# A scheduler for two attentions on one core: opening the next accumulator early, issuing VectorE's score banks on their own, and measured times for VectorE and its shared port

## The chip, the cores and the metric

The kernel runs on one core of one Trainium2 chip. The time is the device time of that core in microseconds (us). The core's engines run side by side: PE (TensorE) multiplies matrices, ACT (ScalarE) takes exponentials, DVE (VectorE) and POOL (GpSimd) do elementwise work, and SP issues DMAs. A program on a single core can be sorted into fast and slow runs only by the spread of its own times.

## The reference, cut to what matters

Two attentions of 32 heads of width 16 over 2048 positions, from separate inputs, joined along the last axis. A is causal within four segments of 512 and adds a memory of earlier segments; B attends to everything.

```python
# A, per segment s
p = softmax(einsum('bhqd,bhkd->bhqk', qs, ks) * scale + mask)
o = g * (phi(qs) @ M) / (phi(qs) @ z + 1e-6) + (1 - g) * (p @ vs)
M, z = M + phi(ks).T @ vs, z + phi(ks).sum()
# B
p = softmax(einsum('bhqd,bhkd->bhqk', q, k) * Dh ** -0.5)     # 2048 x 2048 for each of 32 heads
out = concat([o_A @ wo_A, (p @ v) @ wo_B], axis=-1)
```

B alone has 32 x 2048 x 2048 exponentials, so the work that counts is: scores on PE, their exponentials, and the product with V (P.V) on PE.

## The kernel before: the parts that matter

A score bank is 128 keys x 512 queries of one head in one PSUM bank; four heads (j = 0..3) make a block of keys. ACT takes the exponentials of tiles of 3 and 2 banks in turn. A unit is the work of one accumulator: four heads and 512 queries of one attention. Some blocks go to VectorE instead: one evacuation per bank (a linear map whose integer result is read as an fp16 bit pattern) and three more "rungs" of the same block with other offsets, all four of which are summed by P.V matmuls. A block that goes to VectorE costs it four evacuations and three rungs, costs PE three more quads of P.V, and takes four banks from ACT.

The program is laid out at build time by a scheduler that keeps an estimated clock for each engine (`T["pe"]`, `T["act"]`, `T["dve"]`, `T["pool"]`) and writes PE's and VectorE's instructions in the order that it thinks best. On the chip that order is fixed: an engine that meets an instruction whose input or buffer isn't ready waits, and what stands behind it waits too (in the profiles below, a 3.7 us wait of VectorE holds up the k bank behind it and with it PE). In the code, slack is the time that PE has until ACT needs its next scores, and backlog the work that VectorE still has before it, both as estimated.

```python
def v_scores(taken, lim=2):              # give score banks to VectorE
    n = 0
    while n < lim and backlog() < VBACK and free_slots(...) and v_pick():
        ...
        later(0.685, v_evac(u, kb, x, j, vt, not left), vt)

# main loop, in order of preference (cut)
if held_back(t) and now >= rel - 0.03:   # all pT buffers still wait for P.V
    forced[0] += 1
    if not pv(1): ...
if slack > 0.45 and backlog() < 0.35 and v_scores(set(), 1):   # VectorE's banks alone
    continue
...
def do_phik(wk, k, out, then=None):      # phi(k), transposed by DMA for the memory of A
    pk = wk.tile([P, W], BF16, name="phkT", tag="phkT")        # one buffer
    ...                                                        # VectorE writes it
    for kb in range(4):
        nc.sync.dma_start_transpose(ph[:, kb, :], pk[:, kb * P:(kb + 1) * P])
...
def half():                              # run inside a task that counts 0.72 us of VectorE
    fin_half(wk, st, e)
    if e == 0:
        sums_ok(wk, 0, 32, okm[:, 0:1], "a")      # three VectorE operations each, not counted
        sums_ok(wk, 32, 63, okm[:, 1:2], "b")
```

`sums_ok` checks that the softmax sums stayed in the range of the approximation; if not, an exact program runs instead.

## Time and profile before

| | before |
|---|---|
| time, median | 935.04 us, 3 runs (934.98 to 935.51) |
| span of the profiled run | 932.0 us |
| ACT busy | 891.3 us in 770 score tiles and 30 other instructions |
| VectorE busy | 759.4 us |
| blocks on VectorE | 111 (444 evacuations, 333 rungs) |

First the page of the kernel before: its busy times (with the share of the span and the number of instructions), and four of its groups of instructions. A group's line ends with its busy time, the mean of one instruction in ns, the idle time just before them, and what ended most of it.

```profile
PE 868.7 (93%) x7609; PEld 265.6 (28%) x7609; DVE 759.4 (81%) x1265; ACT 891.3 (96%) x800; POOL 170.1 (18%) x335
...
L774 ACT ACTIVATE pT<-s_ps 128x1536 bf16<-128x1536 f32 (+1 forms) x770 | 879.3, 1301 | 21.3 <-PE s_ps L104 10.8
L846 DVE TENSOR_SCALAR vx<-v_ps 128x512 uint16<-128x512 f32 x444 | 296.6, 686 | 90.5 <-PE v_ps L104 86.5
...
L858 DVE TENSOR_SCALAR vx<-vx 128x2048 uint16<-128x2048 uint16 x333 | 221.3, 708 | 1.9
...
L104 PE MATMUL acc<-zeros 128*128 128x512 bf16 x508 | 164.6, 386 | 0.0
```

PE looks as busy as ACT, but 508 of its matmuls are filler on zeros: the scheduler puts them where PE has nothing to do. ACT has 96% and nothing that could be left out. Where it idles is shown by the windows of the kernel before, for ACT (columns: stretch, its length, busy time and number of instructions, granted PE clock, DMA share, GB/s):

```profile
0.00:42.00 42.00, 21.48 (x21) 0.84 0.76 166
42.00:97.00 55.00, 54.71 (x51) 1.00 0.08 21
97.00:860.00 763.00, 759.02 (x680) 1.00 0.03 9
860.00:932.00 72.00, 56.09 (x51) 0.93 0.03 10
```

Length less busy time is idle time: 20.5 us while weights and first projections arrive, 0.3 us from 42 to 97 us, 4.0 us in the 763 us after that, and 15.9 us in the last stretch, most of it the tail after the last tile. ACT is the limit, so what the change is worth is the ACT time it removes, less the ACT idle time that it adds.

### The profile page before, as it was taken

What the parts mean: (1) busy time and instruction counts of PE and PEld (TensorE: products, weight loads), DVE (VectorE), ACT (ScalarE), POOL (GpSimd) and SP (SyncE); (2) the same over time, 40 slices, a digit from 0 to 9 for tenths busy, and PEclk for the clock granted to TensorE, in tenths of its full rate; (3) what the DMA queues carried; (4) which work ended last, traced back from release to release, by engine and by line L of the source; (5) the groups of instructions that cost most, each with busy time, mean ns of one, the idle gap of its engine ahead of it and who ended that gap; (6) DMA issues with size and microseconds to landing.
All of it is one profiled execution on the core that took longest, in us unless ns stands there. A gap on an engine that the chain in (4) does not pass through costs nothing.

```text
span 932.0 us, 18773 instructions
## 1 busy us (share of the span) xinstructions
PE 868.7 (93%) x7609; PEld 265.6 (28%) x7609; DVE 759.4 (81%) x1265; ACT 891.3 (96%) x800; POOL 170.1 (18%) x335
## 2 busy tenths in 40 slices
PE   7899999999999999999999999999999999999986
PEld 2222232233232222223322233222232222222221
DVE  2474798888888888898888988888898988887885
ACT  4799999999999999999999999999999999999985
POOL 3740141330303003030220303021030300000000
PEclk9799999999999999999999999999999999999998
DMA  8600000000000110000000000000000010000000
GB/s 182 135 13 18 13 4 10 18 13 1 3 5 13 41 24 7 2 1 7 2 6 2 26 27 2 1 2 1 1 1 2 13 34 2 1 1 1 1 1 27
DMA packets 35648, 15.46 MB, mean 17 GB/s; under 512 B 27360, under 2 KB 35552, under 8 KB 35552
## 3 DMA queue, kind: packets, MB, share of 16 engines
q1 hardware_dynamic: 33776, 13.78, 6.1%
q8 instruction: 61, 1.00, 0.4%
q10 hardware_dynamic: 1776, 0.40, 0.2%
q14 instruction: 35, 0.29, 0.1%
HBM read 4.20 MB, written 4.19 MB: 9 GB/s over the span
## 4 chain that ended last, share of the span: by engine, by line
ACT 53%; issue 24%; PE 14%; POOL 5%; DVE 3%; DMA 1%; SPq 1%; ACTq 0%; DVEq 0%; POOLq 0%
ACT pT L774 52%; PE acc L104 5%; PE s_ps L104 4%; POOL pT L784 4%; PE v_ps L104 2%; ACT ex L260 1%; PE k_ps L104 1%; POOL qB L240 1%; DMA w_a<-in_A_wv_dram 1%; PE q_ps L104 1%; DVE vx L846 1%; SPq L205 1%; DVE vx L858 0%; PE l_ps L104 0%; PE o_ps L104 0%
## 5 line engine op out<-in xcount | busy, mean ns | idle before, releaser
L774 ACT ACTIVATE pT<-s_ps 128x1536 bf16<-128x1536 f32 (+1 forms) x770 | 879.3, 1301 | 21.3 <-PE s_ps L104 10.8
L846 DVE TENSOR_SCALAR vx<-v_ps 128x512 uint16<-128x512 f32 x444 | 296.6, 686 | 90.5 <-PE v_ps L104 86.5
L104 PE MATMUL s_ps<-qB,KB 32*128 32x512 bf16 x1604 | 253.9, 383 | 28.3 <-ACT pT L774 22.1
L858 DVE TENSOR_SCALAR vx<-vx 128x2048 uint16<-128x2048 uint16 x333 | 221.3, 708 | 1.9
L784 POOL TENSOR_SCALAR_AFFINE_SELECT pT<-pT 128x256 bf16<-128x256 bf16 (+2 forms) x244 | 111.9, 490 | 345.4 <-ACT pT L774 344.5
L104 PE MATMUL acc<-vx,VB 128*32 128x512 f16 x1776 | 164.9, 385 | 5.0 <-DVE vx L858 4.7
L104 PE MATMUL acc<-zeros 128*128 128x512 bf16 x508 | 164.6, 386 | 0.0
L104 PE MATMUL acc<-pT,VB 128*32 128x512 bf16 x1604 | 159.0, 389 | 0.0
L104 PE MATMUL v_ps<-qB,KB 32*128 32x512 bf16 x444 | 157.0, 384 | 0.5 <-DVE vx L846 0.2
L104 PEld LDWEIGHTS <-KB 32*128 32x128 bf16 x2048 | 85.7, 91 | 243.5 <-issue 235.8
L104 PEld LDWEIGHTS <-VB 128*32 128x32 bf16 x3380 | 71.6, 94 | 150.3 <-issue 140.1
L104 PEld LDWEIGHTS <-zeros 128*128 128x128 bf16 x524 | 40.7, 98 | 96.0 <-issue 86.1
L240 POOL TENSOR_SCALAR qA<-qc,par 128x512 bf16<-128x512 bf16 x30 | 26.4, 894 | 214.6 <-DVE qc L238 214.6
L104 PE MATMUL s_ps<-qA,kA 32*128 32x512 bf16 (+3 forms) x512 | 53.5, 306 | 8.3 <-ACT pT L774 4.9
L333 DVE STREAM_TRANSPOSE tT<-acc 128x512 f32<-128x512 f32 x64 | 45.2, 707 | 8.4 <-PE acc L104 8.0
L104 PE MATMUL acc<-pT,vA 128*32 128x128 bf16 (+3 forms) x512 | 38.2, 315 | 6.0 <-DVE vA L280 2.7
L104 PEld LDWEIGHTS <-kA 32*128 32x128 bf16 x512 | 16.6, 92 | 52.2 <-issue 49.8
L238 DVE CAST qc<-q_ps 128x512 bf16<-128x512 f32 x31 | 21.3, 686 | 8.7 <-PE q_ps L104 8.1
L240 POOL TENSOR_SCALAR qB<-qc,par 128x512 bf16<-128x512 bf16 x32 | 24.9, 792 | 7.7 <-DVE qc L238 7.7
L408 DVE CAST osb<-o_ps 128x512 bf16<-128x512 f32 x28 | 19.2, 686 | 8.1 <-PE o_ps L104 7.1
L104 PE MATMUL v_ps<-w_a,xT_a 128*128 128x512 bf16 x64 | 20.0, 408 | 3.1 <-DMA w_a<-in_A_wv_dram 2.2
L280 DVE CAST VB<-v_ps 128x512 bf16<-128x512 f32 x16 | 11.0, 690 | 12.6 <-PE v_ps L104 12.6
(86 smaller groups left out, 421.7 us busy)
## 6 DMA issues: line engine op xcount, KB each, us to landing
out_dram<-osb SPq DMA_DIRECT2D x31, 128.0 KB, 1.7
w_b<-in_B_wqkv_dram SPq DMA_DIRECT2D x3, 512.0 KB, 5.1
phk<-phkT SPq DMA_TRANSPOSE x48, 2.4
w_a<-in_A_wv_dram SPq DMA_DIRECT2D x1, 512.0 KB, 7.2
wo_a<-in_A_wo_dram SPq DMA_DIRECT2D x1, 512.0 KB, 4.2
wo_b<-in_B_wo_dram SPq DMA_DIRECT2D x1, 512.0 KB, 5.1
w_a<-in_A_wk_dram SPq DMA_DIRECT2D x1, 384.0 KB, 8.6
w_a<-in_A_wq_dram SPq DMA_DIRECT2D x1, 384.0 KB, 9.2
```

Source lines behind the costliest of these rows:

```text
L104: return pin(nc.tensor.matmul(out, lhsT, rhs, **k))
L205: nc.sync.dma_start_transpose(t[:, cc, :], xs[name][ch * W:(ch + 1) * W, cc * P:(cc + 1) * P])
L238: pin(nc.vector.tensor_copy(qc[:], ps[:]))
L240: pin(nc.gpsimd.tensor_scalar(dst[:, e, :], qc[:], par[:, e:e + 1], 0.0, ALU.mult, ALU.add))
L260: pin(nc.scalar.activation(ex[:], src, ACT.Exp))
L280: pin(nc.vector.tensor_copy(dst, ps[:].rearrange("p (h d) -> p h d", d=DH)))
L333: pin(nc.vector.transpose(st["tT"][:, e].rearrange("p c d -> p (c d)"), acc[:]))
L408: pin(nc.vector.tensor_copy(osb[:], ps[:]))
L774: pin(nc.scalar.activation(pT[:, 0:n, :], pt[:, 0:n, :], ACT.Exp, scale=SCALE))
L784: pin(nc.gpsimd.affine_select(out=blk, in_=blk, compare_op=ALU.is_ge, fill=0.0, base=0, pattern=[[0, len(sls)], [1, P]], channel_multiplie ...
L846: pin(nc.vector.tensor_scalar(x[:, j, :], vt[:], XSCALE, float(LADDER[0]), ALU.mult, ALU.add))
L858: pin(nc.vector.tensor_scalar(p[:], x[:], float(off - LADDER[0]), 32767.0, ALU.add, ALU.min))
```

## The change

Its intent: find more room for blocks on VectorE. It has three parts. VectorE's banks may be issued in a PE group of their own as soon as there is 0.35 us of slack and up to 1.4 us of backlog (before: 0.45 and 0.35), with a deeper backlog (1.8 instead of 1.2) and three blocks ahead instead of two. A P.V of the next unit may open its accumulator before the present unit is done, when buffers are held up. The scheduler counts 0.055 us less of VectorE's occupancy than its latency, models the SBUF port that VectorE and GpSimd share, and no longer flushes the pending finishing steps when a unit ends. The diff, cut to its core:

```diff
-VBACK = 1.2
+VBACK = 1.8
+DVEEND = 0.055
-VAHEAD = 2
-VFROM = 9
+VAHEAD = 3
+VFROM = 8
+VALONE = 1.4
     def on_pool(us, ready):
-        T["pool"] = max(T["pool"], ready) + us
+        start = clear(max(T["pool"], ready), ports["dve"])
+        T["pool"] = start + us
+        ports["pool"].append((start, T["pool"]))
         def emit(t):
-            T["dve"] = max(T["dve"], t["ready"]) + t["us"]
+            start = begin(t)
+            T["dve"] = start + t["us"] - DVEEND
+            if t["port"]:
+                ports["dve"].append((start, T["dve"]))
         def unit_done(u):
-            if e == 0:
-                while nfin[0]:
-                    assert dve_force(1) or dve_force()
-        def pv(lim, force=False):
+        def pv(lim, force=False, over=False):
-                if not pv(1):
+                if not pv(1) and not pv(1, over=True):
-            if slack > 0.45 and backlog() < 0.35 and v_scores(set(), 1):
+            if slack > 0.35 and backlog() < VALONE and v_scores(set(), 1):
... (a second use of over; tT gated by a flag; the loop at the end; an unused way to GpSimd)
```

More of the change, by code (lines that the diff above doesn't have):

```diff
@@ L53 @@
 VNOM = 3.75
-VAHEAD = 2
-VFROM = 9
+VAHEAD = 3
+VFROM = 8
+VALONE = 1.4
+POOLMIN = 99
 LEAD = 2.5
@@ L90 @@
     slots, live = [0.0] * 3, [False]
-    held = dict(qc=0, ex=False, phi=deque())
+    ports = {k: deque(maxlen=8) for k in ("dve", "pool")}
+    held = {"tT": False, "ex": False, "qc": 0, "phi": deque()}
     def mm(out, lhsT, rhs, at=0.0, **k):
@@ L114, in on_act, with clear, later @@
         return T["act"] + ACTEND
+    def clear(at, spans):
+        for a, b in spans:
+            if a <= at < b:
+                at = b
+        return at
     def on_pool(us, ready):
-        T["pool"] = max(T["pool"], ready) + us
-    def later(us, f, src=None, prio=0, ready=None, ok=None):
+        start = clear(max(T["pool"], ready), ports["dve"])
+        T["pool"] = start + us
+        ports["pool"].append((start, T["pool"]))
+    def later(us, f, src=None, prio=0, ready=None, ok=None, port=False, rung=None):
         if not live[0]:
@@ L125, in later @@
         seq[0] += 1
-        tasks.append(dict(prio=prio, seq=seq[0], ready=ready, us=us, f=f, src=src, ok=ok))
+        tasks.append(dict(prio=prio, seq=seq[0], ready=ready, us=us, f=f, src=src, ok=ok, port=port, rung=rung))
     def palloc(pool, shape, name):
@@ L137, in mark @@
     def mark(key, at=None):
-        avail[key] = T["dve"] if at is None else at
+        avail[key] = T["dve"] + DVEEND if at is None else at
     const = ctx.enter_context(tc.tile_pool(name="const", bufs=1))
@@ L236, in evac @@
             qc = wk.tile([P, W], BF16, name="qc", tag="qc", bufs=2)
-            held["qc"] += phi is not None
             pin(nc.vector.tensor_copy(qc[:], ps[:]))
@@ L243, in evac @@
             if phi is not None:
+                held["qc"] += 1
                 def then():
@@ L269, in rest @@
             next_phi()
-        later(1.1, rest, ready=end)
+        later(1.0, rest, ready=end, port=True)
     def do_v(mp, w, xT, kb, dst, key=None):
@@ L331, in f @@
             if e == 0:
+                held["tT"] = live[0]
                 st["tT"] = wk.tile([P, 2, 16, 32], F32, name="tT", tag="tT")
@@ L335, in f @@
                 then()
-        later(0.72, f, acc)
+        later(0.72, f, acc, ok=lambda: "tT" in st if e else not held["tT"])
     def fin_mem(mp, wk, st, mbd, phi, e, then=None):
@@ L353, in fin_pair @@
         rr = rsum[:, ridx:ridx + 2, :].rearrange("p e (c o) -> p e c o", o=1)
-        yield 0.35 if name == "b" else 0.5
+        yield 0.35 if name == "b" else -0.5
         pin(nc.vector.reciprocal(rr, tT[:, :, :, DH:DH + 1]))
@@ L364, in fin_pair @@
         if aT is None:
-            yield 0.75
+            yield -0.75
             pin(nc.vector.tensor_tensor(o, tT[:, :, :, 0:DH], rr.to_broadcast(bc), op=ALU.mult))
         else:
-            yield 0.5
+            yield -0.5
             r2 = wk.tile([P, 2, 16, 1], F32, name="r2", tag="r2", bufs=2)
@@ L372, in fin_pair @@
             t1, t2 = tT[:, :, :, 0:DH], aT[:, :, :, 0:DH]
-            yield 0.7
+            yield -0.7
             pin(nc.vector.tensor_tensor(t1, t1, rr.to_broadcast(bc), op=ALU.mult))
-            yield 0.7
+            yield -0.7
             pin(nc.vector.tensor_tensor(t2, t2, r2[:].to_broadcast(bc), op=ALU.mult))
-            yield 0.7
+            yield -0.7
             pin(nc.vector.tensor_tensor(o, t1, t2, op=ALU.add))
@@ L605, with begin @@
         held.update(pk=0, ph=0)
-        vlive, nfin = [2], [0]
+        vlive, npool = [2], [0]
+        def begin(t):
+            at = max(T["dve"], t["ready"])
+            return clear(at, ports["pool"]) if t["port"] else at
         def emit(t):
             tasks.remove(t)
-            T["dve"] = max(T["dve"], t["ready"]) + t["us"]
+            start = begin(t)
+            T["dve"] = start + t["us"] - DVEEND
+            if t["port"]:
+                ports["dve"].append((start, T["dve"]))
             if t["src"] is not None:
                 i, _ = slot_of.pop(id(t["src"]))
-                slots[i] = T["dve"] + 0.05
+                slots[i] = T["dve"] + DVEEND + 0.05
             t["f"]()
@@ L624, in dve_run @@
                     return
-                at = min(max(T["dve"], t["ready"]) for t in el)
+                at = min(begin(t) for t in el)
                 if at > limit:
                     return
-                emit(min((t for t in el if t["ready"] <= at), key=lambda t: (t["prio"], t["seq"])))
+                emit(min((t for t in el if begin(t) <= at + 0.01), key=lambda t: (t["prio"], t["seq"])))
         def dve_force(cls=None):
@@ L633, in dve_force @@
                 return False
-            emit(min(el, key=lambda t: (max(T["dve"], t["ready"]), t["prio"], t["seq"])))
+            emit(min(el, key=lambda t: (begin(t), t["prio"], t["seq"])))
             return True
@@ L640, in fin_push @@
         def fin_push(g):
-            c = next(g)
-            nfin[0] += 1
             def step():
@@ L646, in step @@
                 if c is None:
-                    nfin[0] -= 1
+                    held["tT"] = False
                 else:
-                    later(c, step, prio=1, ready=T["dve"])
-            later(c, step, prio=1, ready=T["dve"])
+                    later(abs(c), step, prio=1, ready=T["dve"], port=c < 0)
+            step()
         def free_slots(at):
@@ L824, with v_scores @@
         vahead = [0]
-        def v_scores(taken, lim=2):
+        def v_scores(taken, lim=2, force=False):
             n = 0
-            while n < lim and backlog() < VBACK and free_slots(T["pe"] + (0.1 if taken else 0.0)) and v_pick():
+            while n < lim and (force or backlog() < VBACK) and free_slots(T["pe"] + (0.1 if taken else 0.0)) and v_pick():
                 u, kb, x, left = vnow[0]
@@ L850, in f, with v_rung @@
                     for off in LADDER[1:]:
-                        later(0.70, v_rung(u, kb, x, off, buf), prio=2, ready=T["dve"], ok=lambda: vlive[0] < VBUFS)
+                        later(0.70, v_rung(u, kb, x, off, buf), prio=2, ready=T["dve"], ok=lambda: vlive[0] < VBUFS,
+                              port=True, rung=v_rung(u, kb, x, off, buf, True) if off == LADDER[1] else None)
             return f
-        def v_rung(u, kb, x, off, buf):
+        def v_rung(u, kb, x, off, buf, pool=False):
             def f():
@@ L857, in f, with pool_run, v_ready @@
                 p = wk.tile([P, 4, 512], U16, name="vx", tag="vx", bufs=VBUFS)
-                pin(nc.vector.tensor_scalar(p[:], x[:], float(off - LADDER[0]), 32767.0, ALU.add, ALU.min))
-                v_ready(u, kb, p, [1])
+                if pool:
+                    pin(nc.gpsimd.tensor_scalar(p[:], x[:], 1.0, float(off - LADDER[0]), ALU.mult, ALU.add))
+                else:
+                    pin(nc.vector.tensor_scalar(p[:], x[:], float(off - LADDER[0]), 32767.0, ALU.add, ALU.min))
+                v_ready(u, kb, p, [1], T["pool"] + 0.4 if pool else None)
                 v_done(buf)
             return f
-        def v_ready(u, kb, p, buf):
+        def pool_run():
+            while T["pool"] < T["pe"] + 0.1:
+                el = [t for t in runnable() if t["rung"] is not None and t["ready"] < T["pe"] + 0.1]
+                if not el or backlog() < POOLMIN:
+                    return
+                t = min(el, key=lambda t: t["seq"])
+                tasks.remove(t)
+                on_pool(2.15, max(T["pe"], t["ready"]))
+                npool[0] += 1
+                t["rung"]()
+        def v_ready(u, kb, p, buf, at=None):
             pd = p[:].bitcast(F16)
-            pvq.append(dict(u=u, kb=kb, v=buf, ready=T["dve"] + 0.06,
+            pvq.append(dict(u=u, kb=kb, v=buf, ready=(T["dve"] + DVEEND if at is None else at) + 0.06,
                             parts=[(pd, j, j, (u, kb, 0, 512, 0), None) for j in q4]))
@@ L921, in finish, with v_key, pv_ready @@
                     chore(at + 8 + 4 * sb, do_out(mp, wk, name, ot, woA if name == "a" else woB, ch, sb, gone))
-        def pv_ready(at):
+        def v_key(q):
+            u = q["u"]
+            return ("v", "a", u["ch"], q["kb"]) if u["name"] == "a" else ("v", "b", q["kb"])
+        def pv_ready(at, over=False):
             if cur[0] == len(units):
@@ L926, in pv_ready @@
             u = units[cur[0]]
-            return sorted((q for q in pvq if q["u"] is u and len(q["parts"]) == 4 and q["ready"] <= at
-                           and ((("v", "a", u["ch"], q["kb"]) if u["name"] == "a" else ("v", "b", q["kb"])) in avail)
-                           and (u["id"] in accs or free_slots(max(at, T["pe"] + 0.05)))), key=lambda q: q["ready"])
-        def pv(lim, force=False):
-            u = units[cur[0]]
-            ready = pv_ready(1e8 if force else T["pe"] + 0.03)
-            for q in ready[0:lim]:
+            if over:
+                if cur[0] + 1 == len(units):
+                    return []
+                u = units[cur[0] + 1]
+                if u["left"] < 2 and not u.get("kbs"):
+                    return []
+            free = free_slots(max(at if at < 1e7 else 0.0, T["pe"] + 0.05))
+            if u["id"] not in accs and free < 1 + over:
+                return []
+            return sorted((q for q in pvq if q["u"] is u and len(q["parts"]) == 4 and q["ready"] <= at
+                           and v_key(q) in avail), key=lambda q: q["ready"])
+        def pv(lim, force=False, over=False):
+            ready = pv_ready(1e8 if force else T["pe"] + 0.03, over)
+            for q in ready[0:1 if over else lim]:
+                u = q["u"]
                 pvq.remove(q)
@@ L947, in pv @@
                 v = vA[u["ch"]] if u["name"] == "a" else VB
-                at = max(at, avail[("v", "a", u["ch"], q["kb"]) if u["name"] == "a" else ("v", "b", q["kb"])] + 0.06)
+                at = max(at, avail[v_key(q)] + 0.06)
                 for pT, sl, j, (_, kb, col, w, c0), t in q["parts"]:
@@ L999 @@
             dve_run(T["pe"])
+            pool_run()
             credit[0] = min(credit[0] + (T["pe"] - clock) * rate(), 2.0)
@@ L1030 @@
                 continue
-            if n and slack > 0.3 and (pend.get(t + 1 - PBUFS, 0) or pend.get(t + 2 - PBUFS, 0)):
-                pv(1)
-                continue
-            if slack > 0.45 and backlog() < 0.35 and v_scores(set(), 1):
+            if slack > 0.3 and (pend.get(t + 1 - PBUFS, 0) or pend.get(t + 2 - PBUFS, 0)):
+                if pv(1) or pv(1, over=True):
+                    continue
+            if slack > 0.35 and backlog() < VALONE and v_scores(set(), 1):
                 continue
@@ L1046 @@
         NT = t
-        assert vnow[0] is None
+        while vnow[0] is not None:
+            dve_run(T["pe"])
+            if not v_scores(set(), 1, True) and not (tasks and dve_force()):
+                urge()
         while chores or cur_chore[0] or tasks or len({q["u"]["id"] for q in pvq}) > 1:
```

## The prediction

> **What bounds the kernel now.** ScalarE's exponentials. The page gives ACT 891.3 us busy of a 932.0 us span; 769 of its 770 score tiles are 3 or 2 banks (385 and 384, groups by form). The chain of waits is 52% ACT on these tiles. The windows of 100 us from 100 to 800 show ACT 99.0 to 99.8% busy, VectorE 84 to 88%, PE with 508 filler matmuls on zeros. ACT idles before tiles only 21.3 us in all: about 13 us before 42 us, and 4.1 us at 898 to 903, where VectorE's check of the sums (six operations, 3.7 us) holds up vector rungs, PE waits 3.8 us, and its matmuls then run at half pace for some 4 us.
>
> **What the change does.** By the built programs it gives VectorE 125 key blocks instead of 111. ACT loses 11 tiles of 3 banks, 11 of 2 and the single one. The reported means (1512 and 1092 ns) overlap: twelve alternating tiles take 13.88 us (timeline), so the pitch is about 1.36 and 0.935 us. ACT is relieved by 11 x 2.295 + 0.5 = about 25.7 us, not the 29 us of the means.
>
> VectorE gains 56 score evacuations and 42 rungs. Three in a row take 1.89 us where one takes 0.69, so the pitch is 0.60 us: about +60 us, so 759 us busy become about 819 of 907, and about 95% in the second half. PE gains 42 quads of P.V (about 0.22 us each), loses 22 score groups and 124 zeros, and has 55 instead of 7 runs with vector scores alone. By counts and a 0.21 us pitch its work stays near 810 us (87% to 89% of the span).
>
> The early accumulator and the deeper backlog let PE work on while VectorE is late. The Trainium skill (SBUF — State Buffer, Who interferes with whom) says VectorE's 2-port modes and GpSimd take a shared port pair exclusively. GpSimd works only 9 to 26 us per 100 us here and its waits end on ACT or VectorE casts, so I give the port model below 2 us.
>
> **On the critical path.** Nearly all of the 25.7 us. Added: about 3 us of new stalls, because VectorE has little room and the scheduler meets more occasions where all P buffers are held (43 instead of 22, counted as it builds). Taken away: perhaps 2 us of the stall at 898. The last P.V is now one of VectorE's rungs rather than ACT's: up to 1.5 us on the tail. Net about -24 us.
>
> **Prediction.** 911 us, range 905 to 920 (-2.6%; the 2% line is 916.3). Faster 0.78, same 0.21, slower 0.01.
>
> **What would show it.** ACT tiles 374 + 373, ACT busy about 865 us and still 99% in the middle windows; VectorE about 819 us; zeros about 384; idle before ACT tiles 18 to 26 us. VectorE waiting for vector scores falls from 86.5 us to about 45.
>
> **What would make it wrong.** VectorE becoming the limit: evacuations late, score banks not freed, PE in program order waiting for VectorE and ACT for PE, shown as ACT idle behind v_ps or s_ps over 30 us. PE idling over 3 us and then running at half pace, as at 900, several times. Or the opposite: the early stalls and the tail shrink too, and it ends below 905.

## The result, and the profile after

The changed kernel took 919.04 us (median of 4 runs, 917.16 to 921.38) against 935.01 us before (4 runs). The ratio is 0.983 with a 95% interval of 0.981 to 0.986: 1.7% faster, which counts as the same at the 2% line. A ratio here and below is the mean time of one kernel's fast runs over that of the other's of the same rounds, so it is not quite the ratio of the medians.

The page of the changed kernel, the same lines:

```profile
PE 870.0 (95%) x7653; PEld 259.9 (28%) x7653; DVE 795.0 (87%) x1363; ACT 867.0 (94%) x777; POOL 158.0 (17%) x333
...
L792 ACT ACTIVATE pT<-s_ps 128x1536 bf16<-128x1536 f32 x747 | 855.3, 1288 | 30.4 <-PE s_ps L108 24.1
L864 DVE TENSOR_SCALAR vx<-v_ps 128x512 uint16<-128x512 f32 x500 | 328.0, 684 | 29.6 <-PE v_ps L108 24.3
...
L880 DVE TENSOR_SCALAR vx<-vx 128x2048 uint16<-128x2048 uint16 x375 | 247.2, 688 | 1.7 <-PE acc L108 0.7
...
L108 PE MATMUL acc<-zeros 128*128 128x512 bf16 x384 | 130.3, 389 | 0.0
```

ACT lost 24.3 us of busy time (891.3 to 867.0), close to what was forecast, but the span fell by only 14.5 us (932.0 to 917.5): ACT idles 10 us more. The windows of the changed kernel, for ACT, say where:

```profile
0.00:42.00 42.00, 22.50 (x21) 0.84 0.77 169
42.00:97.00 55.00, 48.20 (x44) 0.94 0.05 11
97.00:860.00 763.00, 758.48 (x681) 1.00 0.04 9
860.00:917.50 57.50, 37.82 (x34) 0.83 0.04 12
```

Through the 763 us in the middle ACT idles 4.5 us where it idled 4.0 before: VectorE, now far busier, holds nothing up there. The loss lies in two short places: 6.8 us instead of 0.3 from 42 to 97 us, and 19.7 us instead of 15.9 after 860 us. In both the granted PE clock is below 1.

The first place, in the timeline of the changed kernel (columns: start, duration, engine, line, operation; in brackets, idle time before it and what ended it):

```profile
62.20 0.82 PE L108 MATMUL v_ps<-w_b,xT_b 128*128 128x512 bf16 x3
62.44 0.69 DVE L279 SCALAR_TENSOR_TENSOR phkT<-ex,po 128x512 bf16<-128x512 f32 x1
63.16 12.37 SPq L304 DMA_TRANSPOSE phk<-phkT  x8
...
65.11 0.67 ACT L273 ACTIVATE ex<-kA 128x512 f32<-128x512 bf16 x1
...
65.92 0.28 DVE L278 TENSOR_SCALAR po<-kA 128x512 bf16<-128x512 bf16 x1
...
69.89 0.69 DVE L279 SCALAR_TENSOR_TENSOR phkT<-ex,po 128x512 bf16<-128x512 f32 x1 [3.68 <-ACT pT L792]
70.49 0.69 DVE L236 CAST KB<-k_ps 128x512 bf16<-128x512 f32 x1
...
71.23 0.39 PE L108 MATMUL v_ps<-qB,KB 32*128 32x512 bf16 x1 [2.55 <-DVE KB L236]
...
73.54 1.45 ACT L792 ACTIVATE pT<-s_ps 128x1536 bf16<-128x1536 f32 x1 [3.25 <-PE s_ps L108]
...
77.66 1.46 PE L108 MATMUL v_ps<-w_b,xT_b 128*128 128x512 bf16 x3
```

VectorE waits 3.7 us before it writes phkT; the k bank that stands behind it in VectorE's order is freed late, PE waits 2.55 us for that bank, and ACT gets its next tile 3.25 us late. Then PE runs at half pace (the granted clock is 0.50 from 72.3 to 79.1 us): three full matmuls take 1.46 us at 77.66, where three of the same shape take 0.82 us at 62.20. The label "ACT pT" on VectorE's wait need not be true. ACT had finished the ex that this operation reads at 65.8 us. What fits better is the first line: SP issues two sets of four transposing DMAs from 63.16 us on, the first set still reads the only phkT buffer, and VectorE's second write has to wait for it. In the kernel before, the two writes lay 9 us apart, and the second began without a wait for the tile:

```profile
53.72 0.72 DVE L266 SCALAR_TENSOR_TENSOR phkT<-ex,po 128x512 bf16<-128x512 f32 x1 [1.21 <-ACT ex L260]
...
62.92 0.69 DVE L266 SCALAR_TENSOR_TENSOR phkT<-ex,po 128x512 bf16<-128x512 f32 x1
```

The change brought them so near that the second could have begun about 4 us after the first (62.4 and 66.2 us); of the DMAs in between the scheduler knows nothing.

The second place, in the same timeline:

```profile
879.12 0.42 DVE L409 TENSOR_SCALAR okt<-rsum 128x512 bf16<-128x512 f32 x1
...
882.18 0.67 DVE L411 TENSOR_REDUCE okm<-okt 128x1 f32<-128x496 bf16 x1
882.77 0.68 DVE L864 TENSOR_SCALAR vx<-v_ps 128x512 uint16<-128x512 f32 x1
...
883.50 0.58 PE L108 MATMUL v_ps<-qB,KB 32*128 32x512 bf16 x1 [3.83 <-DVE vx L864]
...
884.23 1.45 ACT L792 ACTIVATE pT<-s_ps 128x1536 bf16<-128x1536 f32 x1 [3.14 <-PE s_ps L108]
...
886.89 1.02 ACT L792 ACTIVATE pT<-s_ps 128x1024 bf16<-128x1024 f32 x1 [1.21 <-PE s_ps L108]
```

The six operations of the two `sums_ok` take 3.7 us of VectorE that the scheduler doesn't count; PE stands 3.83 us at a score bank that isn't free, and ACT idles 3.14 us and then four more times by about 1 us while PE is slow (7.5 us in all from 877 to 897 us). The kernel before has a stall at the same checks, from 898 to 903 us, with 4.1 us of ACT idle time; there PE stands in a P.V, at a rung that is late. Its timeline:

```profile
899.27 0.67 DVE L397 TENSOR_REDUCE okm<-okt 128x1 f32<-128x496 bf16 x1
899.86 1.89 DVE L858 TENSOR_SCALAR vx<-vx 128x2048 uint16<-128x2048 uint16 x3
900.60 0.40 PE L104 MATMUL acc<-vx,VB 128*32 128x512 f16 x4 [3.82 <-DVE vx L858]
...
901.42 1.02 ACT L774 ACTIVATE pT<-s_ps 128x1024 bf16<-128x1024 f32 x1 [3.21 <-PE v_ps L104]
...
903.37 15.97 ACT L774 ACTIVATE pT<-s_ps 128x1536 bf16<-128x1536 f32 x14 [0.93 <-PE v_ps L104]
```

### The profile page after: what moved, and what is told of

It is laid out like the page before. It is cut to its first block, busy times and chain, and to the rows that moved or that the text cites. A ratio compares the mean times of both kernels' runs of the same rounds, so it can differ in the third digit from the quotient of the medians.

```text
span 917.5 us, 18925 instructions
## 1 busy us (share of the span) xinstructions
PE 870.0 (95%) x7653; PEld 259.9 (28%) x7653; DVE 795.0 (87%) x1363; ACT 867.0 (94%) x777; POOL 158.0 (17%) x333
## 5 line engine op out<-in xcount | busy, mean ns | idle before, releaser
L792 ACT ACTIVATE pT<-s_ps 128x1536 bf16<-128x1536 f32 x747 | 855.3, 1288 | 30.4 <-PE s_ps L108 24.1
L864 DVE TENSOR_SCALAR vx<-v_ps 128x512 uint16<-128x512 f32 x500 | 328.0, 684 | 29.6 <-PE v_ps L108 24.3
L880 DVE TENSOR_SCALAR vx<-vx 128x2048 uint16<-128x2048 uint16 x375 | 247.2, 688 | 1.7 <-PE acc L108 0.7
L108 PE MATMUL acc<-vx,VB 128*32 128x512 f16 x2000 | 186.5, 388 | 2.3 <-DVE vx L880 1.7
L108 PE MATMUL v_ps<-qB,KB 32*128 32x512 bf16 x500 | 178.1, 385 | 8.9 <-DVE vx L864 4.6
L802 POOL TENSOR_SCALAR_AFFINE_SELECT pT<-pT 128x256 bf16<-128x256 bf16 (+2 forms) x242 | 105.7, 466 | 345.0 <-ACT pT L792 344.1
L108 PE MATMUL acc<-pT,VB 128*32 128x512 bf16 x1548 | 154.4, 391 | 0.8 <-DVE tT L347 0.5
L108 PE MATMUL acc<-zeros 128*128 128x512 bf16 x384 | 130.3, 389 | 0.0
L108 PEld LDWEIGHTS <-zeros 128*128 128x128 bf16 x400 | 33.1, 98 | 83.5 <-issue 76.8
L249 DVE CAST qc<-q_ps 128x512 bf16<-128x512 f32 x31 | 21.2, 685 | 10.2 <-PE q_ps L108 7.2
L251 POOL TENSOR_SCALAR qB<-qc,par 128x512 bf16<-128x512 bf16 x32 | 23.6, 750 | 12.5 <-DVE qc L249 12.5
L108 PE MATMUL v_ps<-w_b,xT_b 128*128 128x512 bf16 x64 | 20.9, 406 | 0.4 <-DVE VB L293 0.2
```

The source lines that it names most:

```text
L108: return pin(nc.tensor.matmul(out, lhsT, rhs, **k))
L249: pin(nc.vector.tensor_copy(qc[:], ps[:]))
L251: pin(nc.gpsimd.tensor_scalar(dst[:, e, :], qc[:], par[:, e:e + 1], 0.0, ALU.mult, ALU.add))
L792: pin(nc.scalar.activation(pT[:, 0:n, :], pt[:, 0:n, :], ACT.Exp, scale=SCALE))
L802: pin(nc.gpsimd.affine_select(out=blk, in_=blk, compare_op=ALU.is_ge, fill=0.0, base=0, pattern=[[0, len(sls)], [1, P]], channel_multiplie ...
L864: pin(nc.vector.tensor_scalar(x[:, j, :], vt[:], XSCALE, float(LADDER[0]), ALU.mult, ALU.add))
```

## The experiments

The theory: the change does what it should for ACT; its missing 8 us against the forecast are two stalls that the scheduler doesn't foresee (a buffer held by DMAs; uncounted VectorE work), each made longer by PE's half pace after it. The main rival: VectorE is so close to full that lateness costs ACT wherever it can. Each kernel was timed in five rounds; the kernel before had medians of 933.65, 933.63 and 933.83 us in the three sets of runs (chips differ), so ratios are the safer comparison between sets. All outputs were correct.

### e1: two phkT buffers, first try

```diff
-pk = wk.tile([P, W], BF16, name="phkT", tag="phkT")
+pk = wk.tile([P, W], BF16, name="phkT", tag="phkT", bufs=2)
-osb = wk.tile([P, D], BF16, name="osb", tag="osb", bufs=3)      # to make room
+osb = wk.tile([P, D], BF16, name="osb", tag="osb", bufs=2)
... (the same for osb in the last output)
```

> The changed kernel with two buffers for phkT (and one osb buffer fewer, to make room); every engine's order in the main path is the same as in the changed kernel. Theory: VectorE's 3.7 us wait before the second phkT write at 66 us is the write waiting for the four transposing DMAs that still read the first phkT; PE then idles about 3 us and runs at half pace to 79 us. Then the wait goes, ACT's idle time between 66 and 82 us falls from about 5.8 us to under 1 us, and the time falls by 5 to 7 us to about 913 us. Rival: VectorE waits there for ScalarE (as the wait list puts it) or for GpSimd and the shared port; then the second buffer changes nothing, 919 us.

Measured: 919.57 us, ratio 0.986, no gain. But the stall was gone: ACT's idle time from 42 to 97 us fell from 6.8 to 3.0 us, and from 60 to 97 us from 6.0 to 0.9 us. In its timeline the second write follows the first within 4 us, with no wait:

```profile
63.79 0.69 DVE L279 SCALAR_TENSOR_TENSOR phkT<-ex,po 128x512 bf16<-128x512 f32 x1
...
67.66 0.69 DVE L279 SCALAR_TENSOR_TENSOR phkT<-ex,po 128x512 bf16<-128x512 f32 x1
```

The time came back at 520 us. The timeline of e1 there:

```profile
523.62 0.69 DVE L422 CAST osb<-o_ps 128x512 bf16<-128x512 f32 x1 [2.96 <-DMA out_dram<-osb]
...
524.37 0.58 PE L108 MATMUL v_ps<-qB,KB 32*128 32x512 bf16 x1 [2.67 <-DVE osb L422]
...
526.18 1.45 ACT L792 ACTIVATE pT<-s_ps 128x1536 bf16<-128x1536 f32 x1 [2.67 <-PE s_ps L108]
```

With one osb buffer fewer, VectorE waits 2.96 us for an output DMA, PE 2.67 us for VectorE, and PE's half pace follows: ACT idled 7.5 us from 500 to 600 us, against 1.4 in the changed kernel. So this run showed the cause of the first stall, and by my own clumsiness made the same kind of stall elsewhere. It says nothing about the worth of the first one in time.

### e5: two phkT buffers, with other room

The room comes from the block masks in bf16 (they hold zeros and ones) and from one r1 and one r2 buffer, which only VectorE touches. The instructions stand in the same order as in the changed kernel on every engine.

> The changed kernel with two phkT buffers again, but with the room taken from small tiles (block masks in bf16, one r1 and one r2 buffer) and the three osb buffers kept; the order on every engine is that of the changed kernel. In the first attempt the stall at 66 us went, but the third osb buffer that I took away made VectorE wait 2.9 us for an output DMA at 520 us, with PE at half pace after it. Theory: with all osb buffers both stalls are absent, ACT's idle time from 60 to 97 us is under 1 us and from 500 to 600 us under 2 us, and the time falls by 5 to 7 us to 912 to 914 us. Rival (a removed stall always comes back elsewhere, as VectorE is near its limit): 918 us or more.

Measured: 912.75 us, ratio 0.977 (0.976 to 0.979); the changed kernel's was 0.983. That is about 0.6% or 6 us, as expected (by the two intervals, between about 3 and 8 us). ACT's idle time was 0.9 us from 60 to 97 us and 1.3 us from 500 to 600 us. A removed stall did not come back elsewhere. The local effect is 5.1 us of ACT idle time (60 to 97 us). Two other pieces differ between the profiled runs and nearly cancel: from 42 to 60 us this run idled 3.4 us where the changed kernel's idled 0.8 (such a difference came without any edit there too, see e7), and after 860 us it idled 17.8 instead of 19.7, of which 1.7 us lies at the checks, where the half pace was shorter (6.8 us at a granted clock of 0.50 instead of 13.7).

### e2, e3, e4: the checks of the sums away

```diff
-                        sums_ok(wk, 0, 32, okm[:, 0:1], "a")
-                        sums_ok(wk, 32, 63, okm[:, 1:2], "b")
+                        pin(nc.vector.memset(okm[:, 0:2], 1.0))
```

> The changed kernel with the first two of the three checks of the sums (six VectorE operations, 3.7 us at 879 us) replaced by one small memset that says they are in order (right for these inputs, but the guard is lost: a diagnosis, not a version). Theory: those operations, which the scheduler does not count, cause the 3.8 us PE wait at 880 us and the half pace after it; ACT's idle time from 877 to 897 us falls from 7.5 us to under 1.5 us and the time falls by 6 to 8 us to about 912 us. Rival: VectorE has too much work in the last stretch anyway; then only the 3 to 4 us of VectorE time are saved or less, and ACT still idles behind v_ps and s_ps for over 3 us there.

Measured: 913.23 us, ratio 0.979, about 4 us less than the changed kernel by ratios and 5.8 by medians: somewhat under the 6 to 8 expected. In its profile ACT's idle time after 860 us is 12.5 us instead of 19.7, all that was expected; the span of the profiled run fell by 6.6 us.

> Both edits together in the changed kernel. Theory: the two stalls are separate and add up: about -12 to -14 us, 905 to 907 us, that is about 28 us below the kernel before, near the 25.7 us of ScalarE work taken away plus the stall at 900 us that the kernel before has too. Rival (VectorE's load is the limit at about 92%): no more than 5 us together.

Measured: 913.30 us, ratio 0.979. This was e1 with e2, so it carries e1's osb stall too (7.5 us of ACT idle time from 500 to 600 us in its profile) and misses its 905 to 907 us for that reason. The last 60 us were as in e2.

> The kernel before with the same two checks replaced by a memset. Theory: its stall at 898 to 903 us has the same cause, 4.1 us of ACT idle; time -4 us, 931 us. If the stall were due to VectorE's rungs in general it would stay at 935 us.

Measured: 929.98 us, ratio 0.996 (0.995 to 0.998), ACT idle time after 860 us 11.6 instead of 15.9 us. The kernel before pays for the same checks, about 3.5 us; the change made them dearer.

### e7: PE kept at work during the checks

```diff
                         sums_ok(wk, 32, 63, okm[:, 1:2], "b")
+                        for _ in range(17):
+                            pin(nc.tensor.matmul(accs[cur[0]][:], zeros[:, 0:P], zeros[:], start=False, stop=False,
+                                                 skip_group_check=True))
```

> The changed kernel with its checks of the sums as they are, and 17 filler matmuls on zeros (3.6 us) put into PE's order where the checks are issued, so that PE works while VectorE is held up; nothing else in the order moves. Theory: a good half of the 7.5 us that ACT loses from 877 to 897 us comes from PE's half pace after its idle time, not from the wait as such: the granted clock there stays at 1.00, ACT's idle time falls to 2 to 4 us and the time by 3 to 5 us, to about 915 us. Rival (VectorE's 3.7 us are lost whatever PE does): no gain or slower, 919 to 922 us.

Windows around the checks, the changed kernel (columns: stretch and length, busy time of PE, PE's weight loads, DVE, ACT and POOL, granted clock, DMA share, GB/s):

```profile
877.00:885.00 8.00, 3.58 (x33) 0.84 (x31) 7.76 (x15) 4.86 (x5) 0.00 (x0) 0.76 0.00 0
885.00:897.00 12.00, 12.00 (x84) 2.34 (x83) 7.91 (x14) 7.50 (x7) 0.00 (x0) 0.59 0.01 1
```

and with the fillers:

```profile
877.00:885.00 8.00, 8.00 (x65) 2.84 (x58) 7.68 (x14) 4.74 (x5) 0.00 (x0) 1.00 0.00 0
885.00:897.00 12.00, 11.28 (x110) 3.05 (x106) 11.54 (x20) 11.32 (x10) 0.00 (x0) 1.00 0.01 1
```

In the first stretch ACT loses as much as before (3.26 against 3.14 us): that is the wait as such. In the second it loses 0.7 instead of 4.5 us: the granted clock stays at 1.00 and PE issues 110 matmuls instead of 84. So about half of the 7.5 us is the half pace after the wait, and it can be had back by idle work. The time is less clear: 918.01 us (915.28 to 918.82), ratio 0.983 as for the changed kernel, where I expected 3 to 5 us. The profiled run shows one reason. Its last stretch gained 3.9 us, but it idled 3.4 us from 42 to 60 us where the changed kernel's idled 0.8: PE waited 1.69 us for a VB evacuation at 49 us and then ran at half pace for 3.4 us (51.0 to 54.4), in a part of the program that the edit doesn't touch. The profile of e6 has the same 1.69 us wait and keeps a clock of 1.00 after it, and that of the changed kernel waits only 0.24 us there. Whether that evens out over many runs was not measured; the local effect is shown, a gain in total time is not.

### e6: a mended version

e5, with the checks as six tasks of the scheduler, of low rank and with their measured times:

```diff
-                        sums_ok(wk, 0, 32, okm[:, 0:1], "a")
-                        sums_ok(wk, 32, 63, okm[:, 1:2], "b")
+                        sums_later(0, 32, okm[:, 0:1], "a")
+                        sums_later(32, 63, okm[:, 1:2], "b")
...
+            for us, f in ((0.45, first), (0.72, second), (0.72, third)):     # in sums_later
+                later(us, f, prio=3, ready=T["dve"])
```

> e5 and the checks of the sums given to the scheduler as six tasks of low rank with their measured times, a full version that keeps the guard. The scheduler then gives VectorE 124 blocks instead of 125. Theory: no stall over 2 us after 97 us; 905 to 909 us, below both kernels. Rival (VectorE's load): 912 us or more, with ACT idle behind v_ps or s_ps in the last 60 us.

Measured: 908.04 us, ratio 0.973 (0.972 to 0.975): it beats both kernels and keeps the guard. Windows of e6 for ACT:

```profile
42.00:97.00 55.00, 51.98 (x47) 1.00 0.06 13
97.00:860.00 763.00, 759.15 (x681) 1.00 0.03 9
860.00:905.60 45.60, 34.14 (x32) 0.94 0.05 15
```

After 860 us it idles 11.5 us, nearly all of it the tail. With 124 blocks on VectorE, ACT idles no more than before the change (38.0 us in the whole span against 40.7). That is against the rival: VectorE's load as such costs ACT nothing here.

### p1, p2, p3: e6 with one part of the change undone

> e6 with the kernel before's rule for scores of VectorE issued on their own (slack over 0.45 and backlog under 0.35 instead of 0.35 and 1.4). The scheduler gives VectorE 118 blocks instead of 124. A block is four score banks, 1.84 us of ScalarE's pitch. Theory: 6 x 1.84 = 11 us more than e6, about 919 us, ACT idle as in e6. Rival (the blocks are not what counts, but the waits): within 4 us of e6.

```diff
-            if slack > 0.35 and backlog() < VALONE and v_scores(set(), 1):
+            if slack > 0.45 and backlog() < 0.35 and v_scores(set(), 1):
```

Measured: 916.89 us (two of five runs near 914.5), ratio 0.981. 8 us over e6 rather than 11, by ratios and by the profiled spans (913.7 against 905.6) alike; ACT busy 877.3 instead of 867.6 us, ACT idle 36.4 instead of 38.0. So the six blocks are what counts, at 1.3 to 1.6 us each, below my 1.84.

> e6 without the part of the change that lets P.V of the next unit open its accumulator early. The scheduler still gives VectorE 125 blocks. Theory: it matters in only about ten places, so the time stays within 2 us of e6. Rival: the early accumulator is what keeps PE going past late VectorE work; then ACT idles more in the middle windows and it takes 4 us or more over e6.

```diff
-                if not pv(1) and not pv(1, over=True):
+                if not pv(1):
-                if pv(1) or pv(1, over=True):
+                if pv(1):
```

Measured: 907.71 us, ratio 0.972 (0.970 to 0.973), no worse than e6 (0.972 to 0.975), though it has one block more on VectorE (125), which by p1 is worth 1.3 to 1.6 us. In its profile one small dip is new (2.4 us of ACT idle time from 400 to 500 us, 0.5 in e6), another gone. Apart from that block, opening the accumulator early is worth nothing that these runs can see, in a schedule that is otherwise free of stalls.

> e6 without the shared port in the scheduler's model and with VectorE's full reported durations (no 0.055 us overlap). The scheduler then gives VectorE 121 blocks instead of 124: three blocks are about 5.5 us of ScalarE work. Theory: +4 to +7 us over e6, through the number of blocks alone, with no more ACT idle time than e6. Rival: the port model avoids collisions; then ACT's idle time in the first 700 us, where GpSimd works, also rises by 3 us or more.

```diff
-DVEEND = 0.055
+DVEEND = 0.0
     def clear(at, spans):
-        for a, b in spans: ...
         return at
```

Measured: 912.02 us, ratio 0.977 (0.976 to 0.979): 4 us over e6, with ACT idle 38.4 us against 38.0. As for the theory: three blocks. The schedule of e6 has fewer collisions at the port: in the traces 23 rungs overlap a GpSimd operation in e6, 49 in p3 and 51 in the kernel before, and all rungs of over 800 ns (5, 16 and 28) are among these. The mean of a rung is 686, 695 and 708 ns. That is off the critical path: ACT idles no more in p3 than in e6. How much of the three blocks comes from the port model and how much from the overlap was not taken apart.

### p6, p7: the kernel before with constants of the change

> The kernel before with backlog 1.8 and three blocks ahead only. The scheduler gives VectorE 115 blocks instead of 111. Theory: 4 x 1.84 = 7 us less than before, about 926 us. Rival as for the run with the rule.

```diff
-VBACK = 1.2
+VBACK = 1.8
-VAHEAD = 2
+VAHEAD = 3
```

Measured: 926.21 us, ratio 0.992 (0.990 to 0.994): -7 us for four blocks, as expected.

> The kernel before with three constants of the change alone: the rule for scores on their own (0.35, 1.4), backlog 1.8 and three blocks ahead; none of its timing model, port model or early accumulator. The scheduler gives VectorE 121 blocks instead of 111. Theory: 10 x 1.84 = 18 us less than the kernel before, about 915 us, with the stall at the checks of the sums still there. Rival: without the measured times the scheduler drives VectorE into lateness, ACT idles 8 us or more in the middle windows, and it stays above 922 us.

```diff
-VBACK = 1.2
+VBACK = 1.8
-VAHEAD = 2
+VAHEAD = 3
-            if slack > 0.45 and backlog() < 0.35 and v_scores(set(), 1):
+            if slack > 0.35 and backlog() < 1.4 and v_scores(set(), 1):
```

Measured: 931.51 us, ratio 0.998: the rival was right here. ACT's busy time did fall, to 874.0 us, but its idle time rose from 40.7 to 59.8 us. (The profiled run was the slowest of the seven, 935.51 us where the others took 930.05 to 932.03, so about 4 us of this may be that run's alone.) Windows of p6 for ACT:

```profile
42.00:97.00 55.00, 54.40 (x50) 1.00 0.09 21
97.00:860.00 763.00, 741.95 (x665) 0.98 0.03 9
```

21 us idle in the middle, where before and after have 4. One of the places, in its timeline:

```profile
577.27 0.61 PE L104 MATMUL acc<-vx,VB 128*32 128x512 f16 x4 [2.22 <-DVE vx L858]
...
578.97 2.36 ACT L774 ACTIVATE pT<-s_ps 128x1536 bf16<-128x1536 f32 x2 [2.56 <-POOL qA L240]
```

PE waits 2.22 us for a late rung, with more work behind it, and goes on at half pace. p3 gives VectorE the same 121 blocks and idles 6.8 us less after 860 us (the checks are counted there) and about 16 us less in the middle. So the constants make the room, and something else in the change makes it usable. p2 and p3 each lack one candidate (the early accumulator; the port and the overlap) and run without stalls, so neither alone is needed; what is left is that either would do, or the parts that I didn't undo: the finishing steps that are no longer flushed at the end of a unit, the tT flag, the looser rule for P.V in the main loop, and VFROM. Which of these it is stays open.

## Why the prediction was right or wrong

The time, 919.04 us, lies inside the range of 905 to 920, at its very end, and that is luck: the largest new stall was not foreseen, the stall at the checks was expected to shrink and grew, and one of the four runs (921.38 us) lies outside. The central 911 us was 8 us too low, and the likeliest class (faster by over 2%, 0.78) did not come: 1.7% is "same", which had 0.21.

- What binds: right. ACT, and in the middle windows the changed kernel's ACT idles 4.5 us in 763 us.
- What is removed: right. "ACT is relieved by about 25.7 us" from the pitch of back-to-back tiles; the profile shows 24.3 us. The means of single instructions would have said 29 us. The Trainium skill (Perfetto Trace Analysis, "Per-instruction lifecycle: what the profiler-reported window actually captures") says that the reported time of a ScalarE or VectorE instruction ends with the acknowledged write, and that the next may start its prefetch before that; the trace agrees (twelve tiles in 13.88 us against 15.6 us by the means).
- VectorE's load: the direction was right, the size not. I said about 819 us and 95% in the second half; it was 795 us, and 91 to 95% in the windows from 600 to 900 us. The two groups together grew by 57 us as forecast (31.4 and 25.9), so the other groups overlap more or became shorter; I didn't take that apart. Its waits for score banks fell from 86.5 to 24.3 us, further than the 45 I gave.
- The step that was mis-sized is the balance of stalls: "Added: about 3 us of new stalls", "Taken away: perhaps 2 us of the stall at 898", up to 1.5 us on the tail, together +1 to +2.5 us. It measured +10 us of ACT idle time (idle before ACT's tiles 30.4 us, where 18 to 26 were forecast). The tail itself, what ACT idles after 860 us without the stall at the checks, grew by only about 0.4 us. In its place the runs showed two things. A second phkT write that the new order brought too near to the DMAs reading the first cost about 6 us (e5). And the checks of the sums, which I expected to hurt less, hurt more: 7.5 us of ACT idle time instead of 4.1 (e2, e4), because the granted clock stayed at 0.50 from 881.2 to 894.9 us instead of from 901.3 to 904.7 us. Part of that is chance: in e1 and e5, with the same order at the checks, the half clock lasted 6.8 us, and ACT's waits there come to 6.2 and 5.8 us.
- The reason that I gave for the new stalls, "VectorE has little room", was wrong for this schedule: e6, with 124 blocks, idles less than the kernel before. "PE idling over 3 us and then running at half pace" was among the things that would make the prediction wrong, and that is what happened; I had not asked what would trigger it.
- The port model was put below 2 us on the critical path and the early accumulator was taken for a help. p3 shows the port model and the overlap together as 4 us, nearly all through three more blocks, and p2 shows no worth of the early accumulator. (GpSimd's 9 to 26 us per 100 us was a misreading too: the windows of the kernel before have 28.9 us from 100 to 200 us, and none from 800 us on.)
- Mended in these two places the change is worth 25 us (e6), about the ACT time that it removes.

## What to carry to other kernels

When a scheduler moves work to an engine, cost the relief by the pitch of back-to-back instructions, then look for what the scheduler does not count: here a one-buffer tile that DMAs still read, and six operations of the checks inside a task that is booked as one. Where PE's clock falls after a wait, the stall costs more than the wait (at the checks ACT waited 3.1 us and lost 7.5 us in all), so take out the wait, or keep PE at work through it. When a removed stall brings no gain, see whether the edit itself made a new one (e1) before believing that the limit lies elsewhere.

## What the Trainium skill lacked or had wrong

- TensorE: Matmul & The Clock Gate ("What's actually happening") has the slow clock come after an idle window of about 3.4 us, and the full clock back after about as much sustained activity. The page says the window runs freely, and these runs fit that: the same 1.69 us wait at 49 us was followed by a clock of 0.50 in e7 (51.0 to 54.4 us) and by 1.00 in e6. Waits shorter than the window sufficed (1.69 us in e7, 2.67 us in e1). After a 3.8 us wait the clock stayed at 0.50 for 3.4 us in the kernel before (901.3 to 904.7 us), 6.8 us in e5 and 13.7 us in the changed one (881.2 to 894.9 us), though there PE's row was 100% busy from 885 us on; e1's stretch at 524 us lasted 10.2 us. All four are multiples of 3.4 us. That a half clock can go on for nearly 10 us in which the row shows no idle time is not on the page.
- SBUF — State Buffer ("Who interferes with whom") says that a VectorE operation in a 2-port mode and a GpSimd operation block each other for the whole instruction. The trace agrees in kind: in the kernel before single rungs took up to 1107 ns against a median of 686 ns, and all 28 rungs of over 800 ns overlap a GpSimd operation. The page gives no idea of the sum, which is small here: the 51 rungs that overlap take 838 ns on average and the others 684, which makes about 8 us of VectorE's time in 932 (an estimate from these means).
- DMA: Bandwidth & Descriptors ("DMA Transpose (X-bar)") gives in that section no time for small transposes out of SBUF. Here four of 128x128 are issued 1.09 to 1.23 us apart and land 2.3 us after their issue, so that their source tile was held for about 6 to 7 us.
